# Attention and gated convolution: plain float32 for seven groups and twelve pairs' scores, with a new order of all steps

## The chip, the cores and the metric

The kernel runs on one core of a Trainium2 chip. The metric is the device time of one execution in microseconds, as a median of three runs. Engines are named as the profile names them: PE (TensorE), DVE (VectorE), ACT (ScalarE), POOL (GpSimd), SP (SyncE, which only issues DMAs here).

## The reference

q, k and v have 8 batches, 12 heads, 448 tokens and 64 columns. All in float32:

```
scores = q @ k.T / 8 - log(448)            # per batch and head
attn   = 1 / (1 + exp(-scores)) ;  x = attn @ v        # heads side by side: 768 columns
gate   = sigmoid(sum over 5 taps of conv_w[k] * x shifted by k tokens)
out    = (gate * (x @ w_val)) @ w_out
```

## The kernel before

Two heads of a batch are a pair (48 pairs), two pairs are a group (24 groups, index j), three groups are a batch. A pair's keys are cut into three chunks of 128 tokens and a remainder of 64; the remainders of a group's two pairs are worked on together.

TensorE multiplies in one of two ways. Plain: float32 operands, each product issued as two instructions. Split: each operand is cut into a high and a low part in a shorter format, and three products replace one. `WHOLE` names the groups whose values (attention times v) are plain, `WHOLE_SCORES` the pairs whose scores are. A split pair needs `split_qk`: the high part as a cast on DVE or ACT (lines 395, 391), the low part as a subtraction on GpSimd (line 404). A split group needs more:
- `scores_rest`: the maximum of the group's values on DVE (line 590), a product of ones with it on TensorE (line 595) ahead of the products of the remainder (line 598), and its exponent on DVE (line 603);
- `v_scale`: the high and low part of v (lines 641, 642);
- `attention`: the sigmoid in place (line 611), then its high part on ACT (line 399) and the residual on DVE (line 622), where a plain group has the sigmoid alone;
- `attend`: three f16 products (lines 661, 669) instead of one float32 product.

After a group's `attend`, `after` copies the result out of PSUM, takes its maximum (line 717) and makes the convolution from taps: some are added by DVE (line 738), some are scaled on ACT, DVE or GpSimd (lines 399, 401) and added by a DMA that GpSimd issues (line 742). The two products with w_val and w_out follow batch by batch, in three f16 products each (line 1053), or for later batches by a scheme with fewer products (line 978), which needs sums of blocks of the gated values (`form`, line 914, on DVE or GpSimd) and of the weights (`mix`).

Buffers come from rings: score banks `ps_a` 3, `qk_src`, `qk_hi`, `qk_lo` and `v_src` 2 each. A new load waits until the last user of the buffer two places earlier is done; `load_v` (line 534) issues group j's values on SP, so it waits for group j-2's `attend`.

The order is written out. The code registers 2717 steps, each with the engines that may do it. `ORDER` names them two characters at a time, in the order of issue, and `ENGINES` gives one letter to each: P, V, A, G, S for TensorE, DVE, ACT, GpSimd and SP. Each engine does its own steps in that order. A GpSimd step that uses the port it shares with DVE also waits for the last DVE step of that kind named before it.

On TensorE the order is: scores of group j+1's pairs ahead of group j's values, as

```
scores(2j+2), scores(2j+3), scores_rest(j+2), attend(j+1), scores(2j+4), ...
```

with the products of the finished batches between them.

Of the kernel before, what the change touches and what calls it, by code (L numbers as in the profile page):

```python
# [37 lines left out]
WHOLE = {0, 1, 2, 3, 4, 5, 6, 7}  # L38
WHOLE_SCORES = {0, 1, 2, 3, 4, 5, 6, 7, 8, 9, 10, 11, 12, 13, 14, 15}
# [74 lines left out]
    "6c5v7N5Q7P7O7x7Q7S0p7R6x0o7T7b7y7V6t7U7Y6u7W8-6U7Z90be6V6y7+95916vbf7X7-80929V6z81826A93836T7z94846W7A9p0r987B"
    "9q856X7C9r6d868i1e8999878j8a9s7D8b6Y9t888k9u8l6Z7E9b8c7c7F8m6B7G8d9cca8e7d7H8n8fbg9v8g9w9y5M9z9x9A9a9E9C8o8r1g"
    "0q9G8s9D9H8A7I8B9d7h1faX8t9F7Je98C7ebh8u9f7f7K8D6+9J8E1h9g8Fbi8p8vbj9I9e8w9Kbk8x8G9M8y0s9h9L1i7i9N9R7g1k9S9Obl"
    "abbm9P1jacbn9i9T7L1l9Qbo9jag0u9W8hbpfmahaj0tai7jam8J1mak8z8K9l8L9Z9X9m8H8S7k8Tal8Man9k9Bad8q8U1nbq8Nap9Y7l8Oaq"
    "8V7mbrae8Waoea8X1o9+asaraY8Iat8Pauav8Y1pcfaJ8Qcg9naDawaxco8RaG1qchaf8ZciaEcp9-cja1ayaMbscqa28+craHfna0csazaFct"
    "btaKckaIa3aNbua4bvaP1raO0vbwc9esaQaU0xbxetaVcbaLaR1sa5aSbyaWcleuaTcuaAbBaZbCaBbEbDa+1tbHcGa6bNa70wcHa-aCbKcxev"
    "cybz1ubFcza8ewcAbIexcI1veycBbJez9ocJeAcCbOeBb0cKbGeCbLcLbPb1bM1wb4bQeDcDa9bRbSeEcMcFcPb2cnc0cYeFcmb5bWcEcZb3cv"  # L120
    "cQbXcwbTd+b6cRbZc+bY1xb+cSbAcT1yc1c-bUeGd0bVc2c3eHd1b-cUc51Ad-eIc41ze1cVe2e0b7gze6eKc6cWcNe3e70Ae4eJk6c7eLeM0y"
    "e8fFe5cXd2cOePc8ebd3eQeNeRecfGd5b8edeeeSd6b9ccfHdcefeTeOd7fId8bafJ0DddeUeYfKdeeVd9eg1CdafLaafMdf1DfNeWdgdb1Bdh"
    "bbeXdoeZfO0zdpdieil1e-k7e+1Edjf0ejfPgAbcf1cdf2ehdqdkf5ekdvf3fbdr1FfQdwdlf8dxf6dsdtf9f7fRdy1Gf4dzdmdAdubddnfcfa"
    "elfe0BfddBemg0d4fjgo1Iffg3dCenfgfkfX1HfYcefh1Jg4flfieodD0Cg5dOfog1fZf+fpfSg2gcdEg9dHg6dIfrg7dJdF1KfsdPgafqg8dK"
    "1MgfdLf-1Ll2dQggdRgb0GfTepgdfvgh1NgegidMftgjdSdNdGgldTgkgp1O1PdUgrgm0EgqdVgsgwfugngtgxdWgugyeqgvdXgXgBgYg+gSgZ"
    "dYh1hydZhzg-hAhChDgDhBgChE1Q1ShGhFhHh4hIgTh7h0hK1RhLhJhMh2gUhO1T0FhPhNfwhQh5h3hUhVh8hWfyh6h9fxgVhahX1UhchbhRhg"
    "i2hSgWi3hji4hYjXi50JhZfUhhh+iahdh-ibhk1Vhiici6hmi7hli8jYhnfzj+jZ0Hhehok3fAj-i1i0k4gEhThfk0kpgFi9kqk1gGhp1Wkrk5"
    "k21X1Ykuk8kskvkxkS1ZkwidiekafBktif0IigkAiiihijkyikfCioilipfDkB1+iqfVisirkDit20kCiuiyivizkEgIiAkziCiDeriEkFkGgJ"
    "fWkHkJiBkIgHkbiGiFkMiH22iI1-iKk9iJiL21kKiMiOiNiPgKkNiQkLiUkPiVgLiWkOkThrkckVkQkUiRkWhqiTk+imkXiwgMkR0MkYk-0KiX"
    "lYhtl0kZlpl3lk23gNhulqlslrllhsiYltiZj2lykdpvj3lvhvgOi+lNj424gPj5lwlm26j6lui-25j7lzlxj9lZ28ln0LlBinlAlClEj8lDgQ"  # L130
    "27lojafEjbl40PlH29jlqqlFjcl5hwkfjdhxkelKjmlGlIjnlL2ajelJ2ckglO2bkhlQlP0NmflVkilRjfgRmgjglSlWlMlTjhkjlXlUmkjipk"
    "l+mlmnl-mmjomomwjsmtklkkjpmhm0mpmxjjjq2djtmqjrqrpw0OjujkmrjvmujwmsjE2emvmijx2gmyjyl6mzmBjz2fmAmjmFjFjAmGjGjLla"
    "l7mHjH2hmIjIjB2ijMmJjNmLmKjJ2kjCplmCl8mMpn0Qpml9jOkmixpOj1mDjKpsjPjD0SmNjQ2jptmXjRmYpT2lpujSpopWknpPjT0Rm1ppmE"
    "jUpXpqprjVm-pxmZpQpYpUjWm+m2pVqfpZq3n0lbq0n1pzpRlcn3n2n42mp+n5pAn7pSn8n6n9q1nbnancldq6p-ndnhniq7q2njq42o2nneq5"
    "q9nk2pnlq8nrqanm2qns2rnnqb2sqcntqgpBqdqiqh0TqJleqnqjj0m3iSlfqoqenfqklgmOqlpynoqm2tqpnqqOnpqsm40UqPqRngquqKqQmP"
    "nunvqSnw2urlnx2vqUnz0VnynAqTnBnDnCnEqVqLnFlhnHnGnIqMlim5nJnNnKnOqX2wnPnRnQqYnSqWnTnXnUnYqZnZn-n+o0m6mQo1q+mSqN"
    "m7q-r1r0ra2xo3r4o4o2o5r7o7o6o8r2pCo9oboaocr5odm8r3ohkooiojr6rbr8m9rd0Wr9remarcpDrirfqtrmmbrgrjok2yrhrkrJrnoerK"
    "rEmRrMrLolrN2CuUommTonmcorrSrFos2zrpmdrorPotouoo2ArVljoqov0YmUrGrOoyrQ2EnVozrTpEowpFrHoAmVoxpGoB2DrUrW2BoCrRoD"
    "rXoEpHrYr+rZs5rIoKs8oLr-oF0-s2ogoMs0oG0XoNmenLoHoRoppIvPoSs3nWoTmWpJs1pKs4oOoI2FoPuJoUsbuVoJoQoVpLvEoWs6p1oXp2"
    "qvoYp3scs9p4oZp52Gqwp82Ho+p9papbs7o-2IuKsauM2J0Zp6wKuLqzuRpMofvbpcvcqxnMuSpdvQ0+p7p0uNpeuTpfuOuPpgrqqAuQphvguW"  # L140
    "vhvjpiviskvkpjslsmvmsosnsprr2KsqvdssqysrstvpsuvlswqBsxsvsyrsvnsAsBszvqqCsCvosGsHvesIsDvs2MvrvtvvsJvuvfvwsKsLvy"
    "rtsM12sQqDsRsNsSvzqFsUqEsTsVsWvB2LsYsX2NsZvAs+t0s-qGt1sdvxt2t4t52Ot3t6vFvCt72QwzvHsf10vIt9vGuZvMsOvDt8vJvNsFsg"
    "vKsP2PsEruvOvL2RwbvRuXqH11wcwewdsewhtatb2Swftcw6tetdtfwkrvtgtkuYw7thw8rwtltmwitotn2UtppNwgtqtstttrwjtuwltwtxw9"
# [1121 lines left out]
```

## Time and profile before

| | us |
|---|---|
| three runs: median (lowest, highest) | 561.56 (560.7, 561.85) |
| the profiled execution: span from its first to its last instruction | 559.5 |
| TensorE busy | 554.8 |
| DVE busy | 487.4 |
| ACT busy | 429.7 |
| POOL busy | 200.8 |
| DMA, mean over the span | 159 GB/s |

The span counts from the program's first instruction to its last; the runs are timed around the whole execution, which adds what lies before and after: 561.56 is 2.0 us more than the span, and the three runs are 1.2 to 2.3 us above it. A busy time is the union of an engine's instructions; matmuls overlap, so the mean length of one is more than its share. The chain of waits is followed back from the last instruction, and each of its pieces names the engine and line that the end then stood on.

### The profile page before, as it was taken

What the parts mean: (1) busy time and instruction counts of PE and PEld (TensorE: products, weight loads), DVE (VectorE), ACT (ScalarE), POOL (GpSimd) and SP (SyncE); (2) the same over time, 40 slices, a digit from 0 to 9 for tenths busy, and PEclk for the clock granted to TensorE, in tenths of its full rate; (3) what the DMA queues carried; (4) which work ended last, traced back from release to release, by engine and by line L of the source; (5) the groups of instructions that cost most, each with busy time, mean ns of one, the idle gap of its engine ahead of it and who ended that gap; (6) DMA issues with size and microseconds to landing.
All of it is one profiled execution on the core that took longest, in us unless ns stands there. A gap on an engine that the chain in (4) does not pass through costs nothing.

```text
span 559.5 us, 10606 instructions
## 1 busy us (share of the span) xinstructions
PE 554.8 (99%) x4061; PEld 325.1 (58%) x4061; DVE 487.4 (87%) x844; ACT 429.7 (77%) x572; POOL 200.8 (36%) x211
## 2 busy tenths in 40 slices
...
GB/s 294 298 306 282 202 264 145 206 129 130 176 188 148 133 97 199 110 208 136 74 177 169 148 175 147 128 150 190 94 158 127 158 100 169 77 76 134 74 36 154
DMA packets 40371, 89.04 MB, mean 159 GB/s; under 512 B 14976, under 2 KB 21248, under 8 KB 40320
## 3 DMA queue, kind: packets, MB, share of 16 engines
...
## 4 chain that ended last, share of the span: by engine, by line
PE 99%; ACT 0%; DVE 0%; issue 0%
PE ps_m L1053 34%; PE ps_a L575 19%; PE ps_a L669 17%; PE ps_m L978 15%; PE ps_a L978 7%; PE ps_a L598 4%; PE ps_a L661 3%; PE ps_m L1096 1%; PE ps_m L463 0%; ACT y_mixed L399 0%; PE ps_a L764 0%; DVE ones L1089 0%; PE ps_m L761 0%; PE ps_a L463 0%; PE ps_a L595 0%
## 5 line engine op out<-in xcount | busy, mean ns | idle before, releaser
L1053 PE MATMUL ps_m<-xs,w_val_hi 128*128 128x512 f16 x504 | 150.1, 379 | 0.0
L611 ACT ACTIVATE ps_a<-ps_a 128x896 f32<-128x896 f32 x112 | 99.5, 907 | 16.5 <-PE ps_a L575 9.8
L742 POOL DMA_DIRECT2D gate<-tap x60 | 53.5, 892 | 152.9 <-DVE gate L738 37.3
L622 DVE SCALAR_TENSOR_TENSOR a<-ps_a,a 128x896 f16<-128x896 f32 x96 | 101.9, 1082 | 3.6 <-ACT a L399 3.5
L1053 PE MATMUL ps_m<-xs,w_val_lo 128*128 128x512 f16 x252 | 95.5, 379 | 0.0
L404 POOL TENSOR_TENSOR qk_lo<-qk_src,qk_hi 128x448 fp32r<-128x448 f32 (+1 forms) x64 | 72.2, 1133 | 63.3 <-DVE qk_hi L395 11.5
L399 ACT ACTIVATE a<-ps_a 128x896 f16<-128x896 f32 x96 | 86.7, 921 | 0.6
L1053 PEld LDWEIGHTS <-w_val_hi 128*128 128x128 f16 x504 | 47.8, 98 | 56.0 <-issue 6.4
L978 PEld LDWEIGHTS <-mixed 128*128 128x128 f16 x648 | 62.4, 98 | 13.0 <-issue 3.7
L611 ACT ACTIVATE a_single<-ps_a 128x896 f32<-128x896 f32 x56 | 47.5, 925 | 11.1 <-PE ps_a L575 6.3
L978 PE MATMUL ps_m<-form,mixed 128*128 128x256 f16 x432 | 54.2, 273 | 0.0
L669 PE MATMUL ps_a<-a,v_hi 128*64 128x448 f16 x384 | 52.7, 354 | 0.0
L399 ACT ACTIVATE tap<-x,cw 128x512 f32<-128x512 f32 x62 | 44.4, 729 | 2.2 <-DVE x L720 2.2
L1053 PEld LDWEIGHTS <-w_val_lo 128*128 128x128 f16 x252 | 24.7, 98 | 29.7
L575 PE MATMUL ps_a<-qk_single 64*128 64x448 f32 x192 | 39.6, 558 | 0.0
L575 PE MATMUL ps_a<-qk_hi 64*128 64x448 f32 x192 | 39.5, 407 | 0.0
L669 PE MATMUL ps_a<-a_single,v_src 128*64 128x448 f32 x192 | 37.8, 543 | 0.0
L978 PE MATMUL ps_m<-form,w_out_hi 128*128 128x256 f16 x216 | 37.6, 273 | 0.0
L738 DVE SCALAR_TENSOR_TENSOR gate<-x,cw,gate 128x512 f32<-128x512 f32 x48 | 36.3, 760 | 0.1
L978 PEld LDWEIGHTS <-w_out_hi 128*128 128x128 f16 x324 | 31.2, 98 | 8.6 <-issue 1.8
L575 PE MATMUL ps_a<-qk_lo,qk_hi 64*128 64x448 f32 x192 | 35.4, 362 | 0.0
L575 PE MATMUL ps_a<-qk_hi,qk_lo 64*128 64x448 f32 x192 | 35.3, 361 | 0.0
...
## 6 DMA issues: line engine op xcount, KB each, us to landing
...
```

Source lines behind the costliest of these rows:

```text
L399: nc.scalar.activation(to, x, AF.Copy, scale=by)
L404: engines[eng].tensor_tensor(to, x, y, op=ALU.subtract)
L575: mm(b()[:, h, :S], k()[rows, at : at + P], q()[rows, :S], start=(n == 0), stop=(n == len(terms(i)) - 1))
L598: mm(b()[to, h, :S], x[n]()[rows, CW:], x[n]()[rows, :S], start=True, stop=True)
L611: nc.scalar.activation(to, b()[:, :, :S], AF.Sigmoid, bias=-math.log(S), scale=1.0 / math.sqrt(D))
L622: op({"V": 1.0}, t + 0.5, lambda e: nc.vector.scalar_tensor_tensor(part(1), p(), A_SCALE, part(0), op0=ALU.mult, op1=ALU.subtract), [b], [ ...
L661: mm(px()[to, p, :S], v()[rows, h * D : (h + 1) * D], x(s["a"])[rows, h, at : at + S], start=(j > 0 and n == 0), stop=(j == 0 and n == len ...
L669: mm(px()[to, p, :S], v()[:, o : o + D], x(st[2 * j + p]["a", c])[:, h, at : at + S], start=(j == 0 and c == 0 and n == 0), stop=(j > 0 an ...
L738: op({"V": 0.67}, at + AT["tap_step"] * k + AT["tap_pair"] * p, lambda e, p=p, part=part, k=k: nc.vector.scalar_tensor_tensor(part(), x()[ ...
L742: op({"G": 0.95}, at + AT["tap_step"] * k, lambda e, tap=tap: nc.gpsimd.dma_start(g(), tap(), accum_op=ALU.add), [tap], [g], 4 * P * T * 4 ...
L978: mm(to(), stat[a](), src()[:, f, :], start=(first and c == 0 and j == 0), stop=(c == NQ - 1 and j == 2), skip_group_check=True)
L1053: mm(po()[:, cs], w()[:, c, :], x(k)[:, cs], start=(c == 0 and j == 0), stop=(c == NC - 1 and j == 2))
```

## The change

`WHOLE` loses group 7 and `WHOLE_SCORES` loses pairs 12 to 15. So pairs 12 to 15 get `split_qk` and three-part scores, and group 7 gets all steps of a split group. Group 6 (pairs 12 and 13) has split scores with plain values. The first loads of plain pairs take turns on three rings up to the first split pair, now pair 12. The two strings are new throughout: 2754 steps in another order, some on other engines.

```diff
-WHOLE = {0, 1, 2, 3, 4, 5, 6, 7}
-WHOLE_SCORES = {0, 1, 2, 3, 4, 5, 6, 7, 8, 9, 10, 11, 12, 13, 14, 15}
+WHOLE = {0, 1, 2, 3, 4, 5, 6}
+WHOLE_SCORES = {0, 1, 2, 3, 4, 5, 6, 7, 8, 9, 10, 11}
 FIRST_SPLIT = min({*range(NPAIRS + 1)} - WHOLE_SCORES)
...
 ORDER = (
-    "3U004z5e0102030504193s3y3e3f3h3g3i3k3j3l3n3m3o3q3p3N0a3r0608073O473P3t3u3Q1a3v3R3z3S1b3A3V3X3T3B3Y3w3+3Z3C3-41"
...
+    "00013u3v3w023x3A04033y3z3B3D484P3C3G3E413I3J3K053L3O0806073M3N3P3Q3R42433F3H444549464b4c3S3T474e4f4d4h4i4g4k4j"
...
 ENGINES = (
-    "GSGGSSSSSSSSPPAPAPAPAPAPAPSASSSPSPVVPVVPVPVVAPAVPVAPVAPSVASPVAPAPPVVVVPVPAVSASVPAVPASVSPPVASPAPVAVPSASPVSAAVPV"
...
+    "SSPPPSAPSSAAPAGGPPAPSVVSVSSSSVVVVVPPAAPPAPPPVVAAAPPPAAPAASPVVSVSSAPPAVPPGPPAPVAPPPAPSVSVVAPAPAVAPAVVVVVVVPPSPP"
...
```

Read off against the code, the strings give these numbers of steps, before and after:

| steps | DVE | ACT | POOL |
|---|---|---|---|
| all | 791, 772 | 576, 611 | 202, 218 |
| high part of q and k (`split_qk`) | 29, 16 | 35, 56 | |
| low part of q and k | | | 64, 72 |
| taps that a DMA adds | 40, 23 | 62, 77 | 18, 20 |
| high part of the blocks in `form` | 13, 19 | 21, 15 | 2, 2 |
| low part of the blocks in `form` | 22, 27 | | 14, 9 |
| sums of the blocks in `form` (four instructions each) | 17, 10 | | 1, 8 |
| residuals of the sigmoid | 112, 119 | | |

TensorE's steps in the new order around group 6 and 7 are: `attend(5)`, `scores(12)`, a sum for w_out's maxima (line 463), `scores(13)`, the product of line 761, `scores_rest(7)`, `attend(6)`, `scores(14)`. ACT's are: the copy of group 5's result, the first sigmoid of pair 12, a cast of `split_qk(14)`, the second sigmoid of pair 12, the diagonal for line 761, the third sigmoid of pair 12, the sigmoids of pair 13. The last result's DMA is issued by SP, before by ACT.

## Rows read from the trace of the kernel before

**Rows 1.** Page, part 1: busy us, share of the span, instructions.

```profile
PE 554.8 (99%) x4061; PEld 325.1 (58%) x4061; DVE 487.4 (87%) x844; ACT 429.7 (77%) x572; POOL 200.8 (36%) x211
```

**Rows 2.** TensorE's waits, whole span: line, releaser, us in total, times, longest.

```profile
PE ps_m L1096 <- DVE ones L1089: 1.1, 1, 1.1
```

**Rows 3.** Chain, 72 to 122 us: start, length, engine, line, instructions.

```profile
73.01 4.71 PE ps_a L575 x24
77.72 0.91 PE ps_a L598 x8
...
84.21 2.46 PE ps_a L575 x12
...
104.96 0.91 PE ps_a L598 x8
105.87 0.75 PE ps_a L661 x8
106.62 4.66 PE ps_a L669 x24
```

**Rows 4.** Chain, 156 to 164 us: a group that is split.

```profile
156.11 0.00 PE ps_a L595
156.11 0.91 PE ps_a L598 x8
157.02 0.57 PE ps_a L661 x12
157.59 3.53 PE ps_a L669 x36
161.12 2.04 PE ps_a L575 x18
```

**Rows 5.** Busy us (instructions) by engine, 150 to 190 us; granted clock, DMA.

```profile
150.00:190.00 40.00, 40.00 (x281) 20.57 (x279) 38.58 (x66) 39.09 (x52) 21.96 (x23) 1.00 0.73 183
```

**Rows 6.** Groups on DVE: count, busy us, mean ns, idle us ahead.

```profile
L622 DVE SCALAR_TENSOR_TENSOR a<-ps_a,a 128x896 f16<-128x896 f32 x96 | 101.9, 1082 | 3.6 <-ACT a L399 3.5
...
L401 DVE TENSOR_SCALAR tap<-x,cw 128x512 f32<-128x512 f32 x40 | 19.4, 493 | 0.6 <-DMA gate<-tap 0.6
...
L590 DVE TENSOR_REDUCE vm<-v_src 128x1 bf16<-128x896 f32 x16 | 17.3, 1078 | 0.0
...
L490 DVE SCALAR_TENSOR_TENSOR w_val_lo<-w_words,val_scale,w_val_hi 128x768 f16<-128x768 f32 x6 | 6.1, 1010 | 0.6 <-ACT w_val_hi L399 0.6
```

**Rows 7.** Line 914 on DVE: count, ns least, median, most; first, last start.

```profile
L914 DVE TENSOR_TENSOR gate<-gate x68: 412/425/947, 176.2 to 534.4; 128x256 f32<-128x256 f32 x68
```

**Rows 8.** Timeline, 95 to 99 us: start, length, engine, line, shapes [idle].

```profile
96.98 1.14 POOL L404 TENSOR_TENSOR qk_lo<-qk_src,qk_hi 128x448 fp32r<-128x448 f32 x1 [1.96 <-DVE w_out_hi L401]
...
97.42 1.51 DVE L490 SCALAR_TENSOR_TENSOR w_out_lo<-w_words,out_scale,w_out_hi 128x768 f16<-128x768 f32 x1
```

**Rows 9.** Timeline of ACT, 62 to 92 us.

```profile
73.06 0.91 ACT L391 COPY x<-ps_a 128x896 f32<-128x896 f32 x1 [1.68 <-PE ps_a L669]
74.07 4.16 ACT L611 ACTIVATE a_single<-ps_a 128x896 f32<-128x896 f32 x5
78.08 0.43 ACT L399 ACTIVATE diagonal<-eye,x_exp 128x128 bf16<-128x128 bf16 x1
78.37 0.76 ACT L399 ACTIVATE tap<-x,cw 128x512 f32<-128x512 f32 x1
...
87.06 0.55 ACT L391 CAST qk_hi<-qk_src 128x448 fp32r<-128x448 f32 x1
```

**Rows 10.** Issues and landings of v_src: 83 to 86, 50 to 90, all.

```profile
84.25 0.33 SPq L534 DMA_DIRECT2D v_src<-vs  x1
...
DMA to landing us min/median/max: 4.2/4.8/5.6
...
DMA to landing us min/median/max: 3.1/4.7/9.2
```

**Rows 11.** Line 742, whole span: ns least, median, most.

```profile
L742 POOL DMA_DIRECT2D gate<-tap x60: 829/880/1060, 66.5 to 521.4; - x60
```

More of the change, by code (lines that the diff above doesn't have):

```diff
@@ L114 @@
[L114 to L143, printed above, removed]
@@ new lines @@
+    "4l4m4n3U3V3W093X190a3-4I4J4O3Z4K4L5u4M4N4Q4S3+4V4T4U4Y4W4Z4t4o0b404p4X4+4-5n504q515o5t4r4s4u4v4w4x4y4z5p525q5r"
+    "5s5v5x5y5A0c0d4A4B1a4C5B0e5z5C4E1b4a4F58531c544G4H1d5556575D5G5E5F5H656667685I696a595a5M0f6c5b5c5d0h0g6b5N3Y5e"
+    "6e0j6u6v6x6y5f6w6A6B5g6z6C6D6E6F1e6S6T6Y5h4R5j5k5S0i6Z5J6h6i5l5m6d6g6j5O5P6k6U6V6W6X6l1g0k6n6o6f6G5w6-1f6m5T5U"
+    "5Q7f7i7g7h7l5V7j7k6p7o7m7p0l1h6q705W727n7q1i5i1j1k4D6+7K736H5K5R717D1l7E7F7G7H0m7I806I5X6J7J6r780n8174756K0o79"
+    "766s777M7N83829q1m5Y1n5Z5+8c5-86848d1o851p8761at896L9f8a626M887P8b8e8f8g639gau9h0p9n8h5L8i7L648j9i7r9j9k8k8l9o"
@@ new lines @@
+    "601q9p7a9l9m1r6t9O9P9s7Q9J9Q8n8m7O7R7b9U6N8y6O8z6P9r9u8o9R6Q8p8q7s9S9V8r1u9X9Y7V7W1s1t9K7c9L9T8s8A8B8t8u8C6R9W"
+    "8DbPbQ9+9-9M0r9Z0q8v8Ea08Ha1a91vbR8I1w8Jaia2a3a58Q7S8K8R7T1y7Ua67dac8Saa8T7x9N8Uab8V8Lad8w8M9v7Xa71xaeaja87tak"
+    "cLafag7e9walah8Nam1A8xan0saoaqbS8War8Fbw7Yap7ZbTasbUavbV7yaRaSbW7z8OaT1zaU7u7Aa+bX8ZaX7vaV8+1CaM7BaNaOaY8-7+ax"
+    "7C7w1BaWaZ8P1Ea4a-7-909691b0979899eK9z8X9a9b92b1b20u931DaPayb4b38GcQ9cbYbl9Cbf94cRcZ1F8YaQb5b69dbcbdcSbg0tfX1G"
+    "cTc+95c-d01HcUb8bibe9ebZbh9xfY1Ib7d1d2cVbmbobp9AbqcK0vbxbrcM9t9ybnc5bjb+b-9Bbtbkbuc01Jc1bsbvcWcXd39Dcac6c7byc8"
@@ new lines @@
+    "d40xawcbccazdfcgaAb9cdbAd5dgcjdhdic2c3cech9Fc4djdkf19Ebzcmf2f3f4f5cf1K0wckcid6d7d8d9dadbf6clcndc9GbBeLcof71Mdl"
+    "cpcqbaaCdocrcycv1LdpcscBdqdrc9dscY9HctbbdxcwdybCaDaBcuf8dzf9fadtdAdBdCcEaEcxezczcA1NeAdeduaFaGcFbDh80y0A1OcCeB"
+    "eC1QcGcD1PeHeI1RaHdDcIfjfkeDaIeEeFeGeMfoeJfpflfq0zdGfbfcaJfrfdcH1SePdHdIfsdNaKfeffcJfmfnftfgfhdOdPdQcN1TdRfufv"
+    "dJfx1UfydnbF9IeQbGdKdLfw1VdS0DfAfzdFfDfBdMfGbEfieOdTkHfCdUbIdZd+d-fEfH1W1XfJaLe0e1cOe4gebHfMfFe5e6fNdd0BdEfIfP"
+    "fQdVgfggdWghfReNfOfSgwfKfLfUfTgigZfVbLbJfWfZgBeRgCcPgjgkglbKgDdXeSgmgEe2e7gF1+e81Y1Ze920gne3gHbMgGdwlCeagxbNgo"
@@ new lines @@
+    "gyegehgKgIebecgJeigLeTejekengMgN1-gzedf-gQ0CgOgRf+eegPeogTepeqel21dYeWgAgSergUgVbOemesetkIg+0EgWefeuh0h1gXg-h2"
+    "hrhsh3hth5evgYh6h4h7ewi7i822ex23eUi9gphahueyhwiahxhbhyhzhAdvib24hIdmicid0GeV25ifigih0Fieijg0hC26ikiliihBiniohD"
+    "28imipitiuhJiveXhEhdhKhLiq27kwiwixhNiyhviziDiEiFiAiHiIiChFiBhGhRhHiGhUhShVeZeYiJhThMhWiKiLhXgqiMhYiNiO29kxhOky"
+    "e+2ahZgrkzkEkAkF2bkBg40HkCkDgsh9gtgul3kGk+hP0JhQl4kJl5iPiQiRiTg1g2hch+iUl6k-l0i0g5iVl1l2iSirl9iZi+2eiWe-i-j0j1"
+    "j2l7j3la2cl8lcj7j42gj82dj9jajbldjcjdlbg3legvjflD2ff0jgjhlflilgisjejilhlrjjjk2hljlllmlojljnjojmg7jplk0Iln0Mjtg8"
@@ new lines @@
+    "jujvg6lslplulvlwi1lt2ikMhelqlzh-lA2jlxlyl+lBi2lEjwl-2km0m1m4m2m5mmjqm72li3ga0Kg9jDjEjFgbjxjGjHjyjz2mlV2om8jIjA"
+    "hhlWm3malXm6m9mdmbhf2nlYmemgmcmhhijKjLmxlZkLhgjM0Lq4gcmjmfmijN2pjJkNhjjOjPmni4mpmomqjQmkmr2q2s2rmumvmQmsgdmlmt"
+    "0N0PmVmwjCj6hkmWmzjRjSm-hlmXk1hm2umYmZi5kOk2jWjXjYk3lGkPjZk4hn2vmRho2t0OkKlFmAn52wn2j5k5m+j+j-n0jTk6n3n1n62xmS"
+    "mTkQn7jUn4k0n8k7k8n92ynahpnhnek9nfnbi6kRmUjVkkkdninknlkSpVkekfhqnjngkgkhklkikmknko0SiY2z2AmykakTkWkbnmkpkjpWpY"
+    "kqjBqspZkrpXksq1ktp+0Qkcp-q0q2iXnwq3qvkuqw2Bq-jsnxnAnyq6qtqukvkUlHqxqyqQnzqnqoqEncnB2CqpqznC2DjrqqnDnEqBnFnGnI"
@@ new lines @@
+    "nHnJqCnKnMqAqHnNnLnOnSnTkXqIqD2E2FnPnUqr0RmCqFqGnWqKnVqLnXkVnYo0o1qJqNndo2qR0V0TqMkYnnlIqSrirjqTqOnZqUlJqYqVqZ"
+    "qPqWqXo3npr1rnrqlLrkq+2Grorrrpo4o5o6n-o8o9o72HoalMlKocrllNmBnQodoermobno2Ir0rsrtogofohoiojomonrWooopoqorosrwru"
+    "2Jowoxoy2K2Mq5rxn+rvrzrylOlPrC2LrArBotrDoAoBozoCoknRoDoErFrLrEoFoGoIoHoJrGnrrIrJoKoLoMoN0U0YoOrHlRlS2NoSoTq8oU"
+    "rMrOrPrQrRmDq7rNrTlQrUrKoVq9mGmHrVnqrS0WqarYsisjsk2O2Sslsr2ToPsdoWmEmFsesfnslTlU2PkZmIntqbr3oXoY2QmJmK2Uoup0p1"
+    "p2p3mLp4sop5oZsmmMp7spssp8r2rZvisup9papbpcp6pdpjpko-plolpmoQpnsqpqovpr2V2RstsnsgpemNrXsv0XpfpgpopsptswmOsxnuqc"
@@ new lines @@
+    "shszppsyphsGsDqdsEqepupvpwpisHpCmPr4qgpxnvsAsJsBpDpEpF0-sCpJqfpGsFpKsKqhsIpypLwdvjvkvqvlpHpzvrpMpNsLpIpOpAoRsM"
+    "vmvnvovsvtr5qjvpvRpBqkpPvSpQpRvvvT2WvUsVsWpSpTpU0Z2+o+sXsZr-vVvMs+sYvN2-vOvPvWs-t0t1t2t3t42Xt5t6t7t8t9tatbvXtf"
+    "tgtcthqitjtkvYv+ql2Y2Ztitlv-tptqvZvytr300+vu31tmw0w1w2w3r6r7vQtttutvtstxtyw4tzw5twtBw6w7w8tCw9tAtD32tFtEtGr8tH"
+    "werbwgwfwotnr9tLtotetM12vxr+vwwawbsOwcwlwm33rc3410tNx8wntOtIratdwp35whwiwHsPsNwjwkwMwqwPwQwNwSwOtP36tQ37tRtSwR"
+    "tVtWtXtZtJwTt+11tYt-u1u2wV38u0wWwUu3vzs0u5u4u6rdreu739wYw-x0wZx2x3wXw+u9uaubrfu8x5ufwIwJwKuguhwLx6ucujuex1ukul"
```

83 lines of the change are left out of this document (40 added, 43 removed).

## The prediction

> **What bounds the kernel now.** I read three views first: the busy shares of the whole span, the list of TensorE's waits, and the chain of work in two stretches. TensorE is busy 554.8 of 559.5 us [rows 1], and in the whole span it waited for another engine once, for 1.1 us at the start [rows 2]. In the two stretches each piece of the chain begins where the one before ends, and all are TensorE's [rows 3, 4]. So the end is set by the sum of TensorE's work, and a microsecond of it is worth a microsecond, as long as no operand comes late. The granted clock was 1.00 [rows 5], the 2.4 GHz level; nothing in the change stops TensorE for long, so I leave the clock alone. DVE (487.4), ACT (429.7) and POOL (200.8) have time left over the span [rows 1], but little in some stretches: from 150 to 190 us ACT is busy 39.09 of 40 and DVE 38.58 [rows 5].
>
> The trace holds one profiled execution, 559.5 us long; the three runs have a median of 561.56. I make the sum against the span and carry it over with the difference, 2.0 us.
>
> **What TensorE saves.** Rows 3 show groups 6 and 7 as they are now, rows 4 a later group that is already split.
> - Scores of pairs 12 and 13: 24 matmul instructions in 4.71 us now [rows 3]; a split pair takes 18 in 2.04 [rows 4]. Saved: 4.71 - 2 x 2.04 = 0.63.
> - Scores of pairs 14 and 15: 12 in 2.46 for one pair now [rows 3], 2.04 after. Saved: 0.84.
> - Values of group 7: 24 in 4.66 now [rows 3], 36 in 3.53 after [rows 4]. Saved: 1.13. Its remainder: 0.75 now, 0.57 after. Saved: 0.18.
> - Scores of group 7's remainder stay float32, 0.91 both times; the one-column product with the value maximum ahead of them shows as 0.00 [rows 3, 4]. It has to start, so up to 0.1 is possible; I take nothing.
>
> Together 2.78 us, say 2.8. Otherwise the table only changes the order of TensorE's steps. To change between scores and other work costs about 0.1 (a lone pair's 2.46 against half of 4.71 [rows 3]); going through both orders I find about one such change of difference, which I leave to the range.
>
> **What the others pay.** Group 7 adds to DVE seven residuals of 1.08, one maximum of 1.08 and the low part of its values, about as much: some 10 us [rows 6]. The table gives more back: 17 taps of 0.49 [rows 6] and seven of the four-part sums of line 914 (28 x 0.43 = 12 us [rows 7]) leave DVE, and so do 13 casts. I estimate DVE at about 10 us less. GpSimd gets those seven sums, which it can't do faster, and eight subtractions of about 1.1 [rows 8], so 20 to 30 us more. ACT gets 21 casts (0.55 each) and 15 taps (0.76 each), reads seven tiles twice where it read them once (0.9 each), and loses six casts: 20 to 24 us more, about 81% of the span [rows 1, 9]. By these averages all three fit beside TensorE, and I cost them at nothing, except where one product needs one result. That cover is thin where ACT stands at 39 of 40; if it is gone, a microsecond that ACT is late is a microsecond of the end.
>
> **Where a product must wait.** The strings of the table name each step by number and engine, so the order on each engine can be read. After the change TensorE's list runs: values of group 5, scores of pair 12, a weight maximum (four one-column products), scores of pair 13, the product of line 761, scores_rest of group 7, values of group 6. Count from the end of group 5's values as zero: two pairs of 2.04 and the small products, so scores_rest is due at 4.1 to 4.3; I take 4.3.
>
> Group 7 is split now, so its scores_rest begins with the product of the value maximum (line 595). That needs line 590 on DVE, which needs the values that line 534 loads. The ring v_src has two buffers, so this load can't start before group 5's values are done: not before zero. In the trace the load of group 8's values stands 0.04 us behind such an end (84.25 on SP, 84.21 in the chain) [rows 3, 10]. Then it has to land: the median of all 24 such loads is 4.7 us, their shortest 3.1 and longest 9.2; the four issued between 50 and 90 us took 4.2 to 5.6 [rows 10]. With 4.7, the maximum's 1.08 [rows 6] and 0.2 for handing over twice, the product can start at 6.0, and TensorE stands still for 1.7 us. With 4.2 it is 1.2, with 5.6 it is 2.6. Everything on TensorE is queued behind it. On DVE the weight parts and the scale of x are queued behind line 590; the first product that needs them comes some 8 us later. In the kernel before, the first group with a maximum is group 8: its load stands at 84.25 and its scores_rest at 104.96 [rows 3, 10]. The change cuts that cover of 20 us to 4.3.
>
> A second delay lies in the same place. Group 6 keeps its plain sigmoids while its pairs 12 and 13 get faster. ACT's list there: copy of group 5's result, sigmoid, cast for pair 14, sigmoid, diagonal, three sigmoids. The copy takes 0.91 and starts 0.05 behind the values; a sigmoid takes 0.81 from start to start (4.16 for five, of which the last 0.92); the cast takes 0.55, the diagonal 0.43 [rows 9]. The cast must wait for pair 12's last product, at 2.2, since its buffer was that pair's. So the second sigmoid runs from about 2.7 to 3.6, where pair 13's second chunk wants the bank at 2.9: 0.7 late. The third ends at about 4.7, where the third chunk, moved by 0.7, wants it at 4.2: another 0.5. That is 1.2 us, but it lies ahead of the same scores_rest, which is then due at 5.5 and still waits until 6.0. The two don't add; the later one decides.
>
> **Sum.** -2.8 + 1.7 = -1.1: 558.4 us of span, and 561.56 - 1.1 = 560.5 us. For the landing I took the median of all, as it lies within the four nearest. Both ends: landing in 3.1 us leaves ACT's 1.2, so -1.6; 9.2 us gives a stand of 6.2, so +3.4. The head is loaded in nearly the same order, and at the tail SP instead of ACT issues the last result, one hand-over, under 0.1; at nothing.
>
> **The rivals.**
> 1. *The wait is hidden.* The load lands early and ACT's cast doesn't delay. Then all 2.8 us stay: 558.8. Against it: none of the four near loads took less than 4.2 [rows 10], and the cast can't start before its buffer is free.
> 2. *GpSimd holds DVE up: slower.* The table puts eight four-part sums on GpSimd where it had one. A weight residual on DVE (line 490) that began at 97.42 beside a GpSimd subtraction from 96.98 to 98.12 took 1.51 us [rows 8], where its kind takes 1.01 [rows 6]; a part of a sum on DVE took up to 0.95 instead of 0.43 [rows 7]. So a DVE step that meets GpSimd may lose 0.5 us. If each of the 28 parts that move catches one, DVE loses 14 us, more than the 10 it is relieved of. TensorE feels it where DVE's residuals feed the next product with nothing to spare, as from 150 to 190, where DVE idles 1.4 us [rows 5]: from three lost steps there it decides. Eight of the 28 would cost 4 us: 564.5. Against it: 96% of DVE was busy there beside 22 us of GpSimd [rows 5], and TensorE never waited [rows 2].
>  The Trainium skill has this as a rule (SBUF — State Buffer, section "Who interferes with whom"): a VectorE instruction with two SBUF inputs and a GpSimd instruction that reads SBUF exclude each other, and the later one blocks until the first ends. By that rule line 490 stood until 98.12, and this row agrees with it.
> 3. *Keeping DVE off GpSimd's queues is worth something itself*, as the change says. The 60 DMA issues of line 742 took 829 to 1060 ns, median 880 [rows 11]: at best 60 x 0.05 = 3 us of an engine that is idle 64% of the span [rows 1]. The time stays at 560.5, and on this point the change can do what it says and nothing is seen of it.
> 4. *ACT gets full elsewhere.* 20 us more on ACT, part of it where it has 0.9 us idle in 40 [rows 5]; about 1 us late in one stretch gives 561.5.
>
> **How the numbers follow.** A change of under about 0.2% (1.1 us) can't be told from none here; the bounds are 560.4 and 562.7. The forecast, a full saving less the wait for group 7's values, gets 0.57, with a range of its own from 559.9 to 561.4. It sits on the lower bound: with a landing under 4.6 it comes out faster, so 0.27 of it lies there and 0.30 within. Rival 1 gets 0.14 (faster), rival 4 gets 0.17 (within), rival 2 gets 0.12 (slower); rival 3 has no time of its own. So faster 0.41, same 0.47, slower 0.12. The range reaches from rival 1, with 0.2 for the order of the steps, to a landing of 6.8: 558.6 to 562.6. It leaves out rival 2 and the longest landings.
>
> **What would show it.** TensorE's list of waits has an entry of 1.2 to 2.6 us between 75 and 80 us, ahead of the product of line 595 (two lines further down after the change), released by DVE's maximum, and the maximum by the DMA into v_src. Pairs 12 to 15 show about 2.04 us each, group 7's values 3.53, and TensorE's busy sum is 2.8 us less. If rival 1 holds, that wait is missing. If rival 2 holds, several waits for DVE's residuals stand behind 150 us, beside GpSimd's sums. If rival 4 holds, they are waits for ACT. The prediction is wrong if TensorE waits for over 1 us in sum elsewhere, or if its own work shrinks by much other than 2.8.

## The result, and the profile after

The kernel got slower: 568.03 us (567.16 to 568.25) against 561.30 (560.7 to 561.85) for the kernel before on the same chip, a ratio of 1.0115 with a 95% interval of 1.0101 to 1.0129. That is 6.7 us more, where 1.1 us less was forecast. The profiled execution has a span of 566.5 us, 7.0 more than before.

Part 1 of the page after, busy us, share and instructions ([rows 1] before):

```profile
PE 555.7 (98%) x4102; PEld 327.6 (58%) x4102; DVE 482.4 (85%) x804; ACT 453.0 (80%) x612; POOL 226.4 (40%) x248
```

DVE is 5 us less busy, ACT 23 and POOL 26 more. What is new shows in TensorE's waits (us in total, times, longest), of which [rows 2] had one, the 1.1 at the start:

```profile
PE ps_a L597 <- DVE vm L592: 1.6, 1, 1.6
PE ps_m L980 <- DVE y L1003: 1.3, 2, 1.0
PE ps_m L1098 <- DVE ones L1091: 1.1, 1, 1.1
PE ps_a L577 <- DVE a L624: 1.1, 1, 1.1
PE ps_a L577 <- ACT x L401: 1.0, 2, 0.7
PE ps_a L577 <- ACT a_single L613: 0.7, 2, 0.5
PE ps_m L980 <- DVE y L403: 0.3, 1, 0.3
```

(Lines after the buffers stand two further down than before.) The first is the wait that was forecast. The third stood in the kernel before, and the sixth, behind ACT's sigmoids ahead of that wait, is the forecast second delay. The other four were not forecast, and their 3.7 us add up to more than the first two together.

To see all that TensorE lost, waits and slower work alike, I took the time from the first instruction of each of its steps to that of the next, and subtracted the median that the same two kinds of steps, one behind the other, have in the trace of the kernel before. What is left is the loss, in us, by place:

| kernel | 0-60 | 60-100 | 100-180 | 180-260 | 260-end | sum |
|---|---|---|---|---|---|---|
| before | 0.6 | -0.2 | 0.1 | 0.3 | 0.8 | 1.6 |
| after | -0.3 | 4.5 | 1.9 | 4.3 | 1.0 | 11.4 |
| other_max | 0.7 | 1.2 | 3.0 | 4.7 | 1.0 | 10.6 |
| cast_dve | 1.0 | 2.7 | 3.0 | 4.7 | 1.0 | 12.4 |
| three_swaps | 0.9 | 2.6 | 1.3 | 2.5 | 1.0 | 8.4 |
| thin_sums | -0.3 | 4.5 | 1.9 | 6.4 | 1.0 | 13.5 |
| stage7 | 0.6 | 2.2 | 3.4 | 4.7 | 1.0 | 11.8 |
| stage7_swaps | 0.6 | 2.2 | 1.6 | 2.6 | 1.1 | 8.1 |
| all_moves | 0.6 | 2.1 | 2.1 | 6.4 | 1.3 | 12.6 |
| best1 | 0.0 | 3.7 | 1.3 | 3.4 | 1.1 | 9.4 |
| no_gate | 0.2 | 1.9 | 1.8 | 2.7 | 0.9 | 7.6 |
| thin_added | 0.7 | 2.1 | 1.4 | 1.5 | 0.8 | 6.6 |
| thin_both | -0.3 | 1.6 | 0.0 | 1.5 | 0.8 | 3.5 |

(The rows below the second are the experiments. Up to 60 us they differ only by when the first loads land, about 1 us from one execution to the next.) After lost 9.8 us more than before, and TensorE's own work, counted with the same medians, is 2.8 less: 9.8 - 2.8 is the 7.0 of the spans. (How steps are sorted into kinds moves these figures by a few tenths.) So the saving is there as forecast, and two stretches eat it: 60 to 100 us, around group 7, and 130 to 260 us.

**Around group 7.** The timeline of SP and DVE (start, length, engine, line; in brackets the idle time ahead and what ended it):

```profile
72.01 0.33 SPq L536 DMA_DIRECT2D v_src<-vs  x1
78.03 1.09 DVE L592 TENSOR_REDUCE vm<-v_src 128x1 bf16<-128x896 f32 x1 [1.59 <-DMA v_src<-vs]
```

TensorE's timeline at the same place, the rows with idle time ahead:

```profile
75.47 0.47 PE L577 MATMUL ps_a<-qk_hi 64*128 64x448 f32 x2 [0.50 <-ACT a_single L613]
76.57 0.47 PE L577 MATMUL ps_a<-qk_hi 64*128 64x448 f32 x2 [0.22 <-ACT a_single L613]
79.17 0.18 PE L597 MATMUL ps_a<-vm,ones 128*128 128x1 bf16 x1 [1.57 <-DVE vm L592]
```

And the windows behind it (length, then busy us and instructions of PE, PEld, DVE, ACT and POOL, granted clock, DMA share, GB/s):

```profile
80.00:81.00 1.00, 1.00 (x12) 0.34 (x8) 0.96 (x6) 0.00 (x0) 0.00 (x0) 0.50 1.09 205
81.00:82.00 1.00, 1.00 (x8) 0.00 (x0) 1.00 (x5) 0.88 (x2) 0.00 (x0) 0.50 1.05 152
82.00:83.00 1.00, 1.00 (x6) 0.29 (x4) 0.96 (x3) 1.00 (x3) 0.00 (x0) 0.50 0.81 289
83.00:84.00 1.00, 1.00 (x8) 0.42 (x6) 1.00 (x1) 1.00 (x3) 0.00 (x0) 0.99 1.00 417
```

The load took 6.0 us. TensorE lost 0.65 and 0.49 behind ACT's sigmoids and 1.74 for the maximum, and then it ran at a granted clock of 0.50, the 1.2 GHz level, until about 83 us, which cost 1.68 more: 4.5 in all.

**From 130 us on.** Three DVE steps in the timeline of after:

```profile
131.64 1.23 DVE L511 TENSOR_SCALAR o_base<-out_inverse,y_inverse 128x6 f32<-128x6 f32 x1
...
193.29 2.11 DVE L406 TENSOR_TENSOR form<-gate,form 128x768 f16<-128x768 f32 x1
...
212.82 1.84 DVE L403 TENSOR_SCALAR gate<-x,cw 128x512 f32<-128x512 f32 x1
```

And the GpSimd instruction beside each of them:

```profile
131.66 1.14 POOL L406 TENSOR_TENSOR qk_lo<-qk_src,qk_hi 128x448 fp32r<-128x448 f32 x1 [1.08 <-issue]
...
193.42 1.16 POOL L867 TENSOR_TENSOR mix<-mix,w_out_lo 128x384 f32<-128x384 f32 x1
...
213.09 1.27 POOL L406 TENSOR_TENSOR qk_lo<-qk_src,qk_hi 128x384 fp32r<-128x384 f32 x1
```

Undisturbed, these steps take 0.23, 0.96 and 0.48 us (below, three_swaps). Behind each, TensorE stood: 0.93 us at 139.6, 1.61 at 196.5 to 197.5, and at 213.0 to 216.1 1.68, of which the first 0.50 has nothing to do with the held step (TensorE's timeline of after):

```profile
212.96 0.38 PE L980 MATMUL ps_m<-form,w_out_hi 128*128 128x256 f16 x2 [0.33 <-DVE y L403]
...
216.10 0.38 PE L980 MATMUL ps_m<-form,w_out_hi 128*128 128x256 f16 x2 [1.02 <-DVE y L1003]
```

The `y` of the first row was done at 212.4, ahead of the held step of 212.82. Behind the three held steps TensorE so lost 0.93 + 1.61 + 1.18 = 3.7 us.

### The profile page after: what moved, and what is told of

The parts are those of the page before. It is cut to its first block, busy times and chain, and to the rows that moved or that the text cites. A ratio compares the mean times of both kernels' runs of the same rounds, so it can differ in the third digit from the quotient of the medians.

```text
span 566.5 us, 10744 instructions
## 1 busy us (share of the span) xinstructions
PE 555.7 (98%) x4102; PEld 327.6 (58%) x4102; DVE 482.4 (85%) x804; ACT 453.0 (80%) x612; POOL 226.4 (40%) x248
## 4 chain that ended last, share of the span: by engine, by line
PE 56%; DVE 8%; ACT 3%; issue 2%; DVEq 0%
PE ps_m L1055 21%; PE ps_m L980 12%; PE ps_a L980 7%; PE ps_a L577 7%; PE ps_a L671 6%; DVE a L624 2%; PE ps_a L600 1%; ACT ps_a L613 1%; PE ps_a L663 1%; DVE gate L1065 1%; DVE a_rest L624 1%; DVE form L406 1%; DVE x_max L719 1%; DVE gate L740 0%; DVE vm L592 0%
## 5 line engine op out<-in xcount | busy, mean ns | idle before, releaser
L406 POOL TENSOR_TENSOR qk_lo<-qk_src,qk_hi 128x448 fp32r<-128x448 f32 (+1 forms) x72 | 79.3, 1118 | 139.1 <-DVE gate L740 58.3
L613 ACT ACTIVATE ps_a<-ps_a 128x896 f32<-128x896 f32 x119 | 106.5, 908 | 11.9 <-DVE v_exp L605 4.5
L624 DVE SCALAR_TENSOR_TENSOR a<-ps_a,a 128x896 f16<-128x896 f32 x102 | 108.0, 1082 | 2.8 <-ACT a L401 2.4
L401 ACT ACTIVATE a<-ps_a 128x896 f16<-128x896 f32 x102 | 91.6, 918 | 1.6
L401 ACT ACTIVATE tap<-x,cw 128x512 f32<-128x512 f32 x77 | 54.1, 726 | 6.0 <-DMA gate<-tap 4.0
L577 PE MATMUL ps_a<-qk_hi 64*128 64x448 f32 x216 | 44.8, 410 | 2.9 <-DVE a L624 1.1
L613 ACT ACTIVATE a_single<-ps_a 128x896 f32<-128x896 f32 x49 | 41.6, 933 | 4.7 <-PE ps_a L577 3.4
L577 PE MATMUL ps_a<-qk_lo,qk_hi 64*128 64x448 f32 x216 | 39.6, 362 | 0.0
L403 POOL TENSOR_SCALAR tap<-x,cw 128x512 f32<-128x512 f32 x20 | 32.3, 1614 | 11.8 <-DVE tap L403 9.3
L671 PE MATMUL ps_a<-a,v_lo 128*64 128x448 f16 x204 | 36.3, 352 | 0.0
```

Of the source, the lines that this page charges most:

```text
L401: nc.scalar.activation(to, x, AF.Copy, scale=by)
L403: engines[eng].tensor_scalar(to, x, by, None, op0=ALU.mult)
L406: engines[eng].tensor_tensor(to, x, y, op=ALU.subtract)
L577: mm(b()[:, h, :S], k()[rows, at : at + P], q()[rows, :S], start=(n == 0), stop=(n == len(terms(i)) - 1))
L613: nc.scalar.activation(to, b()[:, :, :S], AF.Sigmoid, bias=-math.log(S), scale=1.0 / math.sqrt(D))
L624: op({"V": 1.0}, t + 0.5, lambda e: nc.vector.scalar_tensor_tensor(part(1), p(), A_SCALE, part(0), op0=ALU.mult, op1=ALU.subtract), [b], [ ...
```

## The experiments

All times are medians, each taken beside the kernel before on the same chip. By the 95% intervals of their ratios, about 0.15% or 0.8 us either way, two kernels that lie under some 1.2 us apart are not told apart. Where a step of the table moves, the diff shows its two characters, or the list of one engine.

### Are the three held DVE steps a cause? (three_swaps)

```diff
-...h9xfY1Ib7d1d2cVbmbobp9AbqcK0v...
+...h9xfYb7d1d2cVbmbobp9AbqcK1I0v...
-...gxbNgogyegehgKgIebecgJei...
+...gxbNgyegehgKgIebecgogJei...
-...0GeV25ifigih0Fieijg0hC26...
+...0GeVifigihieijg0250FhC26...
```

> Kernel after, with three GpSimd steps named behind a DVE step instead of ahead of it (each engine keeps its own order, so that all that changes is that GpSimd waits for that DVE step): the low part of pair 19 behind line 511, a part of mix (line 867) behind line 909, the second low part of pair 25 behind line 731. In the profile of after these three DVE steps took 1.23, 2.11 and 1.84 us where their kinds take about 0.2, 0.85 and 0.48, each until a GpSimd instruction ended, and behind each TensorE stood: 0.93 at 139.6, 1.61 from 196.5, 1.68 from 213 to 216. Theory (DVE is held by GpSimd at the shared port, and TensorE feels it): about 4 us less than after, 564, and the three DVE steps back to their usual lengths. Rival (ACT and DVE are full there; what is gained at one place is lost at the next): under 1.5 us less, 566.5 or more, with waits for ACT or DVE in place of those.

Measured: 564.77, 3.3 us less than after. (Against the two executions of after whose mean clock was 1.00, 567.2 and 567.9, it is 2.7.) The three DVE steps in its timeline:

```profile
131.35 0.23 DVE L511 TENSOR_SCALAR o_base<-out_inverse,y_inverse 128x6 f32<-128x6 f32 x1
...
192.17 0.96 DVE L406 TENSOR_TENSOR form<-gate,form 128x768 f16<-128x768 f32 x1
...
211.10 0.48 DVE L403 TENSOR_SCALAR gate<-x,cw 128x512 f32<-128x512 f32 x1
```

And one of the GpSimd steps, which now waits:

```profile
193.22 0.92 POOL L867 TENSOR_TENSOR mix<-mix,w_out_lo 128x384 f32<-128x384 f32 x1 [0.71 <-DVE form L406]
```

Every engine does the same work in the same order, so the meeting itself is a cause: TensorE's waits at 139.6, 196.6 and 216.1 us are gone (of the one ahead of the third held step 0.40 stays). In the table above 2.4 of the 3.3 us are gone between 100 and 260 us; in this profile the clock also stayed at 1.00 behind group 7's wait.

### Is it the sums, as the second rival said? (thin_sums)

```diff
-                    for a, by in SUMS:
-                        engines[e].tensor_tensor(x[:, a, :], x[:, a, :], x[:, by, :], op=ALU.add)
+                    n = HT if e == "V" else 16
+                    for a, by in SUMS:
+                        engines[e].tensor_tensor(x[:, a, :n], x[:, a, :n], x[:, by, :n], op=ALU.add)
```

> Kernel after, with the eight sums of blocks that GpSimd does (line 918) cut to 16 of 256 columns, so that most of that work is left out and the products that use the sums are of other numbers. Theory (it is not these sums that hold DVE up, but GpSimd's subtractions): under 1 us less than after, 567 or more. Rival (the second rival of the prediction: the sums hold DVE up): 3 to 4 us less, 564 to 565.

Measured: 570.14, slower than after by 2.1. That lies in the theory's "567 or more", but a loss was foreseen by neither. With its sums cut, GpSimd comes earlier to its next subtraction, and that meets a DVE cast which it had missed (elsewhere in the table its losses are those of after). DVE, GpSimd and TensorE in the timeline of thin_sums:

```profile
203.53 2.54 DVE L397 CAST form<-gate 128x768 f16<-128x768 f32 x1
```
```profile
203.55 2.11 POOL L406 TENSOR_TENSOR form<-gate,form 128x1024 f16<-128x1024 f32 x1
```
```profile
208.50 0.38 PE L671 MATMUL ps_a<-a,v_hi 128*64 128x448 f16 x2 [1.16 <-DVE a L624]
```

So it isn't the amount of GpSimd's work, nor the sums. One subtraction that comes at the wrong moment holds one DVE step for about as long as it lasts.

### What is group 7's wait worth? (other_max, cast_dve)

```diff
-            m, v = vm.new(), s["v"]
+            m, v = vm.new(), two[6 if j == 7 else j]["v"]
```

> Kernel after, but scores_rest of group 7 takes its maximum from group 6's values, which are loaded long before (so group 7's values are scaled by another group's exponent; that part of the computation is changed). The wait for the load of group 7's values is taken away, nothing else. In the profile of the kernel after TensorE stands 1.74 us longer ahead of this product than its work asks, and the 3.9 us behind it run at a granted clock of 0.50, which costs 1.68 more. Theory (the wait and the lower clock that follows it are a cause): 3.4 us less than after, 564.6, with the granted clock at 1.00 from 79 to 85 us; the two waits for ACT's sigmoids (1.14 us together) just ahead stay. Rival (ACT and DVE are late there anyway, the wait only comes last): under 1 us less, 567 or more, with a wait for ACT in the same place.

Measured: 567.03, only 1.0 less, which is hardly clear of the spread. The wait and the low clock are gone (the windows from 78 to 86 us show 1.00), and 3.3 of the 4.5 us with them. Then TensorE waits again: 0.46 more at 111 us, 0.6 at 173. The theory had the place right and its price wrong. In the kernel after itself, two executions had a mean clock of 0.997 and took 568.2, the two with 1.00 took 567.2 and 567.9. Of the 1.68 us of low clock some 0.7 would so be left at the end; four executions are few for that.

```diff
-...VAPSAPVVV...
+...VAPSVPVVV...
```

> Kernel after, with one letter of the table changed: the cast of pair 14's high part (0.57 us at 74.03 in the profile of after) is done by DVE and not by ACT between two sigmoids. Theory (the two delays ahead of group 7's remainder don't add, the load decides): the waits of 0.65 and 0.49 us for ACT's sigmoids go, the wait for the maximum grows by as much, and the time stays within 0.5 us of after, 568.0. Rival (each delay counts by itself): 1.1 us less, 566.9.

Measured: 568.50, the same within the spread. The wait for the maximum is as long as before (1.73). Ahead of it 0.94 is left of the 1.14, since ACT's second sigmoid stayed late for another reason: the diagonal between the sigmoids waits for DVE, which has the cast now (ACT's timeline of cast_dve):

```profile
76.39 0.40 ACT L401 ACTIVATE diagonal<-eye,x_exp 128x128 bf16<-128x128 bf16 x1 [0.51 <-DVE x_exp L757]
```

### Both causes taken away with all the work kept (stage7, stage7_swaps)

```diff
-        v = two[j]["v"] = v_src.new()
+        v = two[j]["v"] = v_src.new() if j != 7 else form_ring.new(
+            lambda: sb.tile([P, VW], F32, name="v_form", tag="form", bufs=FORMS))
```
```diff
 SP:
+     v of group 7
      qk of pair 14, qk of pair 15
-     v of group 7
 DVE:
-     weight word
+     maximum of group 7
      tap, tap, x_max of group 5
-     second part of the cast of pair 14
      four short steps
+     both parts of the cast of pair 14
      w_out_hi
+     weight word
      maximum of a weight
-     maximum of group 7
 ACT: sigmoid, sigmoid
-     diagonal, sigmoid
+     sigmoid, diagonal
```

> Kernel after, with the delays around group 7 taken away without leaving out work: group 7's values go to a buffer of another ring that is free then, their load is issued ahead of the loads of pairs 14 and 15, their maximum is made earlier on DVE, the cast of pair 14 goes to DVE, and ACT makes the diagonal behind pair 12's third sigmoid. In the profile of after TensorE loses 4.5 us from 75 to 85 us (1.1 behind ACT, 1.7 for the maximum, 1.7 by the granted clock of 0.50 that followed). Theory: these 4.5 us go, and some 1.4 to 2.2 of them are given back at single waits for ACT and DVE from 110 to 200 us, as in the run with the other maximum, which took 3.3 away there and gave back 1.4: 565 to 566. Rival (from 85 us on ACT and DVE set the pace, and what comes early waits): 567 or more.

Measured: 568.62, no gain at all: the rival's figure. From 74 to 78 us TensorE loses 0.2, but at the next pair it loses 1.8, behind the residual of group 7's remainder, which DVE makes late (TensorE's timeline of stage7):

```profile
85.73 0.47 PE L578 MATMUL ps_a<-qk_hi 64*128 64x448 f32 x2 [1.03 <-DVE a_rest L625]
86.97 0.47 PE L578 MATMUL ps_a<-qk_hi 64*128 64x448 f32 x2 [0.37 <-ACT x L393]
```

Part of that may be a fourth meeting, which the new order made itself. The weight word now comes beside a GpSimd subtraction (DVE, then GpSimd in the timeline of stage7):

```profile
76.63 1.91 DVE L452 SCALAR_TENSOR_TENSOR w_words<-w_words 128x768 int32<-128x768 int32 x1
```
```profile
76.43 1.28 POOL L406 TENSOR_TENSOR qk_lo<-qk_src,qk_hi 128x448 fp32r<-128x448 f32 x1 [3.57 <-PE ps_a L578]
```

All twelve steps of its kind take 0.95 to 1.00 us in after, so 0.95 is lost, and from there DVE works without a gap up to the residual at 84.59. By that list up to 0.95 of the 1.8 us may be this meeting; no run takes it away alone. It is in all the kernels below that build on stage7 (1.90 to 1.92 us), best1 excepted.

> The kernel of the run stage7, with the three GpSimd steps named behind the DVE steps that they held up, as in the run three_swaps. Theory (two separate causes): the gains add, 3.3 for the swaps and 2.3 to 3.1 for group 7: 561.5 to 562.5, about the kernel before (561.4). Rival (they share what is given back): 563.5 or more.

Measured: 565.68, 2.9 less than stage7, and no better than three_swaps alone (0.9 more, within the spread). The gains don't add: the swaps keep their worth, and group 7's 4.5 us, taken away in this way, are worth nothing. How the lead is lost shows in when TensorE begins the values of a group, in us later than before (each counted from the scores of pair 2):

| values of group | 6 | 8 | 10 | 11 | 12 | 20 |
|---|---|---|---|---|---|---|
| after | 3.0 | 1.9 | 1.0 | 4.9 | 7.0 | 7.9 |
| three_swaps | 2.3 | 0.4 | -1.4 | 1.5 | 2.9 | 3.7 |
| stage7 | -0.1 | 0.2 | 0.1 | 4.4 | 6.4 | 7.4 |
| stage7_swaps | -0.1 | 0.2 | -1.6 | 1.3 | 2.8 | 3.7 |
| thin_both | -0.1 | -1.3 | -3.9 | -1.7 | -0.3 | 0.0 |

(The steps between two groups stand in another order than before, so a column is compared downwards.) A difference of 2.4 us between three_swaps and stage7_swaps at group 6 is 0.2 at group 8: between them lies the 1.8 us at 84 to 87, for half of which the fourth meeting may stand. So these two runs don't show by themselves that group 7's wait is worth nothing; with other_max, where no such meeting was made and 3.3 us of loss gave 1.0 at the end, it is worth little.

### Single steps, or full lists? (all_moves, best1)

```diff
 ACT:
-tap, copy of result 7      ...  tap, copy of result 9      ...  xs, copy of result 13
+copy of result 7, tap      ...  copy of result 9, tap      ...  copy of result 13, xs
 DVE:
-form low part, residual, residual  ...  x_max, y (k=1)  ...  v_lo, y (k=3)
+residual, residual, form low part  ...  y (k=1), x_max  ...  y (k=3), v_lo
```

(The second of the three swaps is left out here, since its DVE step moves itself.)

> The kernel of the run stage7_swaps, with single steps put elsewhere in an engine's list where in the profile of three_swaps TensorE stood 0.25 to 0.56 us for it: ACT copies the results of groups 7 and 9 ahead of a tap and that of group 13 ahead of a part of x; DVE makes a low part of form behind a residual, and two steps of the first products with the sums ahead of a maximum and of a low part of v. TensorE's own work is 2.8 us less than in the kernel before. Theory (what is left are single steps in the wrong place, not engines that are full): some 2 us less than stage7_swaps, 559.5 to 560.5, faster than before. Rival (ACT and DVE are full from 110 to 250 us, and each wait removed comes back at the next place): within 0.7 us of stage7_swaps.

Measured: 569.07, 3.4 more than stage7_swaps. The moved low part made GpSimd late, and a subtraction met another cast (DVE, then GpSimd in the timeline of all_moves):

```profile
201.87 2.63 DVE L397 CAST form<-gate 128x768 f16<-128x768 f32 x1
```
```profile
201.79 2.13 POOL L406 TENSOR_TENSOR form<-gate,form 128x1024 f16<-128x1024 f32 x1
```

TensorE lost 2.4 us behind it, and the granted clock fell to 0.50 again, from 207.6 us for 3.4 us. Best1 leaves that move out, has all three swaps, and puts group 7's exponent and residual ahead of weight work (with it, GpSimd's low parts of pair 14 are named behind two weight steps, and ACT makes the high part of the remainder ahead of xs):

```diff
 DVE:
-w_out_hi, weight word, maximum of a weight, w_out_lo, x_exp, ..., v_exp 7, ..., xs, xs, residual 7
+w_out_hi, w_out_lo, x_exp, v_exp 7, ..., residual 7, xs, xs, ..., weight word, maximum of a weight
```

> The kernel of the run stage7_swaps with steps moved within DVE's and ACT's lists: from 76 to 88 us the exponent and the residual of group 7's remainder come ahead of weight work (TensorE stood 1.8 us behind them), later the moves of the run all_moves, without that of the low part of form, which let a cast on DVE meet a GpSimd subtraction (2.62 us instead of 0.8) and cost 2.4 us there. Theory (single steps in the wrong place): 1.8 + 1.7 us less, 562 to 563. Rival (ACT is full, and each wait comes back at the next place at the same time after the start): within 1 us of 565.7.

Measured: 566.43, not told apart from stage7_swaps. The place at 85 us is mended, and in the profiled execution 3.4 us are lost from 91 to 101 instead, where the weight maximum is late and the clock falls to 0.50 again. (The other three executions had a mean clock of 1.00 and took 565.4 to 566.8, so the clock is not the reason.) TensorE's timeline, then a window, of best1:

```profile
94.68 0.21 PE L465 MATMUL ps_a<-out_max,ones 128*128 128x1 bf16 x3 [0.70 <-DVE out_max L455]
```
```profile
98.00:100.00 2.00, 2.00 (x7) 0.74 (x6) 1.93 (x6) 2.00 (x4) 1.52 (x2) 0.50 0.04 8
```

### Which list is full? (before_no_gate, no_gate, thin_added, thin_both)

```diff
-        op({"A": 0.95}, t + AT["gate"], lambda e: nc.scalar.activation(g(), g(), AF.Sigmoid), [], [g])
+        op({"A": 0.95}, t + AT["gate"], lambda e: None, [], [g])
```

> The kernel before without the same 21 sigmoids of the gate on ACT. In its profile TensorE stands for no other engine after the start. Theory (TensorE is the bound before the change, ACT has time left): within 0.5 us of the kernel before, 561.4. Rival (ACT sets the pace before the change too): 1 us less or more.

Measured: 561.46 against 561.53, a ratio of 1.0001 (0.9992 to 1.0011). Before the change 22 us of ACT are worth nothing.

> The kernel of the run stage7_swaps (565.7) without the 21 sigmoids of the gate (line 747, 1.05 us each on ACT), so the gate is left unsquashed and that work is left out. In the profile of stage7_swaps TensorE still stands 2.0 us from 80 to 100 us and 4 us in pieces of 0.2 to 0.75 from 100 to 250, mostly for ACT and for buffers that ACT or DVE frees. Theory (ACT is full there, so what comes early waits for it): about half of this goes, 2 to 4 us less, 562 to 563.5. Rival (DVE sets the pace, or single steps in the wrong place): under 1 us less, 565 or more.

Measured: 564.64, 1.0 less than stage7_swaps, hardly clear of the spread: between the two figures, and too little for ACT alone.

```diff
-part(), x()[:, p, :, HALO - k : HALO + SL - k], w(p, k), part(), op0=ALU.mult, op1=ALU.add),
+part()[..., :8], x()[:, p, :, HALO - k : HALO + 8 - k], w(p, k), part()[..., :8], op0=ALU.mult, op1=ALU.add),
```

> The kernel of the run stage7_swaps (565.7) with the 48 taps that DVE adds (line 741, 0.74 us each) cut to 8 of 64 columns of each block, so most of that work is left out on DVE and about 25 us of DVE go. Theory (ACT is full, DVE less so): 0 to 1.5 us less, 564 to 566. Rival (DVE sets the pace): 2 to 4 us less, as is expected of the run without the gate's sigmoids.

Measured: 563.66, 2.0 less. I had put ACT first; DVE's cut gave 2.0 where ACT's gave 1.0, which these runs barely tell apart.

> The kernel of the run stage7_swaps (565.7) with both cuts: the 48 taps that DVE adds are cut to 8 of 64 columns of each block, and the 21 sigmoids of the gate on ACT are left out. One alone gave 2.0 and 1.0 us. Theory (DVE's and ACT's lists are full between 80 and 250 us and hide what TensorE saves; a step of TensorE waits for the later of the two): the two cuts give at least their sum, 3 to 5 us, 560.5 to 562.7. Rival (each cut has taken away what lists can give back, the rest are single places that both leave standing, as the 1.8 us from 85 to 87 us): 563 or more.

Measured: 561.86 beside 561.68 for the kernel before in the same comparison, a ratio of 1.0007 (0.9995 to 1.0018): 3.8 less than stage7_swaps, at least about what the two cuts make singly. (Its profiled execution, 560.3, is the fastest of its ten.) From 100 to 180 us TensorE's loss is 0.0. TensorE's waits in thin_both are down to the start, the one at 85 us and one more (its lines stand one further down than in after):

```profile
PE ps_m L1099 <- DVE ones L1092: 1.1, 1, 1.1
PE ps_a L578 <- DVE a_rest L625: 1.0, 1, 1.0
PE ps_m L981 <- DVE y L403: 0.4, 1, 0.4
```

So what the swaps left of the slowdown hangs on DVE's and ACT's work: with less of it the loss is gone, while the same cut of ACT alone is worth nothing in the kernel before. That their lists from 80 to 260 us are full together, and TensorE's step waits for the later one, is the reading that fits; it is argued, not shown, for the order of their steps would look the same. The windows hint at it: from 80 to 200 us DVE is busy 115.94 of 120 us in the kernel before,

```profile
80.00:200.00 120.00, 120.00 (x763) 58.71 (x761) 115.94 (x200) 111.08 (x153) 56.67 (x63) 1.00 0.65 155
```

and 115.77 after:

```profile
80.00:200.00 120.00, 117.85 (x772) 59.21 (x765) 115.77 (x192) 112.07 (x153) 59.78 (x66) 0.99 0.60 148
```

But the busy share alone doesn't tell whether TensorE waits. In thin_both, with no loss from 100 to 180 us, it is nearly as high:

```profile
80.00:200.00 120.00, 118.96 (x809) 61.27 (x807) 114.51 (x199) 111.50 (x153) 65.52 (x70) 1.00 0.64 156
```

None of these kernels beats the kernel before. The best that does all the work is three_swaps, 564.77.

## Why the prediction was wrong, point by point

1. **TensorE's own work, 2.8 us less: right**, to a few tenths. With all losses taken out, that is the difference.
2. **The wait for group 7's values: right in place and cause, too small.** The landing took 6.0 us, beyond the nearest four on which I rested. From the end of group 5's values the product stood at 79.17 - 71.90 = 7.3 us, not 6.0; ACT's second delay was 1.14 (forecast 1.2), and, as forecast, it only shared the time with the wait: the trace has the maximum waiting for the load. The stand at this product, 1.74, looks like the sum's 1.7 by luck. That 1.7 held ACT's 1.2 as well; ACT's delay and the stand came to 2.9.
3. **The clock, left alone: wrong.** "Nothing in the change stops TensorE for long" goes ill with the sum's own stand of 1.7 us, and what followed the stand cost 1.68 us more, at 0.50. It is not in the sum, though in the end little of it counts.
4. **The others' work at nothing: the step that failed.** The amounts were nearly right for ACT (+23) and POOL (+26). For DVE it was -5 against about -10: the estimate left out the six high and five low parts of `form` that the change's own table moves to DVE, some 9 us by their lengths in after, 0.69 and 0.95 (an estimate). But I set all of them against averages of the whole span. The stretch that decides is 80 to 260 us, and from 80 to 200 DVE got no relief: 115.94 before, 115.77 after. [Rows 5] had hinted at it with 38.58 and 39.09 of 40; I took it for a thin cover and priced it, as rival 4, at 1 us. Where I had put nothing the runs showed two things: the meetings of point 5, 2.7 to 3.3 us, and about 3.4 more, which go when DVE and ACT have less to do (thin_both, 3.8 less than stage7_swaps). That a DVE and an ACT that just kept up with the old TensorE can't keep up with one that is 2.8 us quicker is the likely reason. The prediction's own sign of being wrong, over 1 us of waits elsewhere, came true with 3.7.
5. **Rival 2, GpSimd holding DVE up: the mechanism was right, its carrier and its chance were not.** It got 0.12, at 564.5. Three meetings cost 2.7 to 3.3 us (three_swaps). I had counted how many parts move to GpSimd; what decides is whether a subtraction begins while a DVE step that TensorE needs is due. And I had taken 0.5 us for one meeting from [rows 8], where the GpSimd instruction had run for 0.4 us; one that begins together with the DVE step cost 1.0 to 1.9 us.
6. **Rival 3, a table that keeps DVE off GpSimd's queues:** not seen. The 60 DMA issues (line 744 now) took 842 to 1162 ns, median 870, against 829 to 1060 and 880 before. In the stretch that decides, this table lets three meetings happen that cost DVE 1.0 to 1.4 us each; the costliest that I found in the trace of before was 0.5.

What is left open: of the 3.4 us by which three_swaps is slower than before, the runs show that they hang on DVE's and ACT's work, but not whether its amount or its order costs them, nor which order would give them back. Two attempts by hand each lost elsewhere what they gained. The fourth meeting, in the kernels built on stage7, was not taken out alone.
